# Turning q's features with VectorE's 32x32 transpose instead of TensorE, for seven of nine token blocks

## The chip, the cores and the metric

The kernel runs on one core of a Trainium2 chip. The metric is the device time of one execution in microseconds (us); less is better. A core has five engines that each run their own program in order and wait for one another through semaphores: TensorE (PE, matmuls; the profile lists its weight loads as PEld), VectorE (DVE), ScalarE (ACT), GpSimd (POOL) and SyncE (SP, which here only starts transfers).

## The reference

Three layers in float32, on inputs of batch 8, 8 heads, 576 positions, 64 features:

```python
q_s = exp(q - max(q, axis=-1)); q_s = q_s / (sum(q_s, axis=-1) + 1e-9)
k_s = exp(k - max(k, axis=2));  k_s = k_s / (sum(k_s, axis=2) + 1e-9)
kv = einsum('bhsd,bhse->bhde', k_s, v)
x = einsum('bhsd,bhde->bhse', q_s, kv)     # -> 4608 tokens x 512
h = x @ w_in;  g = where(h > 0, h, exp(min(h, 0)) - 1);  x = g @ w_out     # 512 -> 2048 -> 512
h = x @ w_in2; g = P(h) / (Q(h) + 1e-6);                 out = g @ w_out2  # P, Q: polynomials of h
```

The first line is the softmax of q over its 64 features, and it is the one that the change touches: for x, a token's 64 features have to lie on partitions (they are contracted with kv), while a maximum and a sum over features want them along the free axis.

## The kernel before

The 4608 tokens are nine blocks of 512 (index `j`, 0 to 8). Attention is done per pair of heads (`hp`, 0 to 3), so there are 36 units of q work, n = 4j + hp. Each matrix product of the two feed-forward layers is done as three matmuls on a high and a low part of each operand (L726 to L728 for `x @ w_in`, L768 for `g @ w_out`), each on tiles of 128x512. A step is one 128-wide slice of the hidden dimension: 12 matmuls into `h`, then on the first layer relu (ACT, L832), exp (ACT, L835), elu (DVE, L838), the high part (ACT, L269), the low part (POOL or DVE, L272), then 12 matmuls of L768. The tile `gs` of high and low part has two buffers; `h` takes one of four PSUM banks.

The q work of a pair (`pair_fns`, `plan_q`) in a 128x512 tile `qt`, with 128 tokens on the partitions and 4 tokens x 2 heads x 64 features along the free axis: `load_q` (SP), `q_max` (DVE, L480), `q_sub` (POOL, L483), `q_exp` (ACT, L487), `q_sum` (DVE, L491), `q_rec` (DVE, L494 and L495), `q_mul` (POOL, L498). Then `q_T`: four TensorE transposes of 128x128 into one PSUM bank (L504), and `q_copy` (ACT, L509), which brings that bank to the tile `qT`. For every second pair, `x_mm` (PE, L545) multiplies two `qT` tiles with their kv matrices, and `x_hi` and `x_lo` make the `xs` tiles that the first layer reads.

Blocks 0 and 1 are done ahead of and beside the first steps (`plan_pair`). For blocks 2 to 8, `plan_late` joins the TensorE part of three pairs in one operation, the `unit` (`plan_unit`): `q_T` of the present pair, the transposes of k's maxima for two later pairs (L442, L450), and the 10 small products that make kv (`kv_mm`, L464). For block 8, which has no k of its own, the unit holds `q_T` alone.

What stands where in each engine's program is set when the program is built, by a planner (class `Plan`). Each operation has an engine with an estimated cost, the operations that it follows, the buffers that it takes and frees, and a rank; the planner starts next what can start first by these costs, and the rank decides between equals. The ranks of the q work of pair n come from `at_step(n)`, counted in steps. The engines then run in that order, whatever the real durations are.

Of the kernel before, what the change touches and what calls it, by code (L numbers as in the profile page):

```python
# [161 lines left out]
def linear_attention_elu_rational(  # L162
# [239 lines left out]
    def pair_fns(n):  # L402
# [69 lines left out]
        def kv_div(e):  # L472
            if e == "ACT":
                nc.scalar.activation(out=kvd[n % 8], in_=b["pk"][:, 0:D], func=AF.Copy, scale=b["rs"])
            else:
                nc.vector.tensor_scalar(out=kvd[n % 8], in0=b["pk"][:, 0:D], scalar1=b["rs"], scalar2=None, op0=ALU.mult)

        def q_max(e):
            b["mx"] = at.tile([P, 8], F32, tag="mx", name="mx", bufs=4)
            nc.vector.tensor_reduce(out=b["mx"], in_=b["qt"], op=ALU.max, axis=AX.X)  # L480

        def q_sub(e):
            engine[e].tensor_tensor(out=b["qt"], in0=b["qt"], in1=b["mx"][:, :, None].to_broadcast([P, 8, D]),  # L483
                                    op=ALU.subtract)
# [140 lines left out]

    def plan_unit(n, q_ready=None):

# [19 lines left out]
        need, free, take = [in_ops[tiles[int(r)]]], [], ["bank"] if any(has) else []  # L647
        if has[0]:
# [9 lines left out]
        if q_ready:  # L658
            need.append(q_ready)
            free.append(("qt", mine["q_op"]))  # L660
            take += ["bank", "qT"]
        u = chain("unit", (PE(0.15 + 0.1 * has[0] + 0.1 * has[1] + 0.65 * has[2] + 0.4 * bool(q_ready)), unit, need, r + 1),
                  take=take, free=free, extra=0.2)
# [11 lines left out]
        if has[2]:  # L675
# [3 lines left out]
            done.append(o)  # L679
        if done:  # L680
            at_ops.append(op((("", 0.0),), lambda e: None, done, r, free=[("bank", u)]))
        if q_ready:
            at_ops.append(op((("", 0.0),), lambda e: None, [mine["qc"]], r, free=[("bank", u)]))

    def plan_late(j, hp):
        n = j * NP + hp
        if n == 2 * NP:
            for m in (n, n + 1):
                plan_k(m)
                plan_unit(m - 2)  # L690
        if n + 2 < B * NP:
            plan_k(n + 2)
        r = at_step(n)
        plan_unit(n, plan_q(n, r - 1, in_ops[tiles[int(r) - 1]], AHEAD))
        if hp % 2:
            plan_x(n, r, [state[n - 1]["qc"], state[n]["qc"]])
# [355 lines left out]
def _laid_out(name, a, np):  # L1052
# [49 lines left out]
```

## Time and profile before

| what | value |
|---|---|
| time, median of 3 runs (lowest to highest) | 1616.13 us (1616.03 to 1617.8) |
| time of the profiled execution | 1616.44 us |
| its span, first to last instruction | 1614.7 us |
| TensorE busy, share of the span | 1584.6 us, 98% |
| VectorE, ScalarE, GpSimd busy | 979.9, 1018.6, 772.0 us (61%, 63%, 48%) |
| mean granted TensorE clock | 0.995 of full speed |

The profiled execution takes 1.74 us more than its span, and lies 0.3 us above the median. The matmuls overlap one another, so the duration of one (mean 379 to 383 ns for 128x512) is longer than the distance from its start to the start of the next; what one costs TensorE is that distance.

### The profile page before, as it was taken

How to read it: one execution, taken by the hardware profiler on the slowest of the kernel's cores; microseconds unless marked ns; L12 is line 12 of the kernel's file. 1: busy time of each engine (PE TensorE's matmuls, PEld its weight loads, DVE VectorE, ACT ScalarE, POOL GpSimd, SP SyncE). 2: the span in 40 equal slices, each digit the busy share in tenths (PEclk: the TensorE clock that was granted, in tenths of full speed). 3: DMA queues.
4: the chain of work that ended last, by engine and by line, in shares of the span. 5: the costliest groups of instructions: out<-in, count | busy, mean ns of one | idle time of the engine just before them, and what ended most of it. 6: DMA issues, size and time to landing. Idle time of an engine off the chain costs nothing.

```text
span 1614.7 us, 21797 instructions
## 1 busy us (share of the span) xinstructions
PE 1584.6 (98%) x8040; PEld 1364.2 (84%) x8040; DVE 979.9 (61%) x1390; ACT 1018.6 (63%) x1688; POOL 772.0 (48%) x562
## 2 busy tenths in 40 slices
PE   6999999999999999999999999999999999999998
PEld 4788888888888888888888888888888888888886
DVE  7897655445344444321125777776868677777676
ACT  6766544454454544443557777777777777777675
POOL 3334333333233322333566666666566666666554
PEclk9999999999999999999999999999999999999999
DMA  8522533232233222110433010101000010100000
GB/s 322 203 118 89 166 120 103 100 114 86 102 102 115 85 92 81 61 40 14 124 93 103 8 53 1 52 1 39 15 26 28 20 34 10 43 8 21 1 27 26
DMA packets 48778, 114.82 MB, mean 71 GB/s; under 512 B 5664, under 2 KB 5664, under 8 KB 46624
## 3 DMA queue, kind: packets, MB, share of 16 engines
q1 hardware_dynamic: 48096, 112.10, 20.1%
q8 instruction: 63, 1.03, 0.3%
q10 hardware_dynamic: 576, 1.33, 0.2%
q14 instruction: 43, 0.35, 0.1%
HBM read 84.05 MB, written 29.36 MB: 70 GB/s over the span
## 4 chain that ended last, share of the span: by engine, by line
PE 87%; issue 4%; ACT 4%; DVE 2%; POOL 2%; DMA 1%; POOLq 0%; SPq 0%; DVEq 0%; ACTq 0%
PE acc L768 42%; PE ps L726 14%; PE ps L728 14%; PE ps L727 14%; POOL gs L272 2%; PE ps L464 1%; PE ps L545 1%; PE ps L504 1%; ACT p L871 1%; ACT s L867 1%; ACT m L877 0%; DMA hc<-w 0%; DMA kt<-in_k_dram 0%; ACT m L880 0%; PE acc L464 0%
## 5 line engine op out<-in xcount | busy, mean ns | idle before, releaser
L726 PE MATMUL ps<-xs,w_in 128*128 128x512 f32 x1152 | 438.8, 381 | 1.8 <-DVE p L892 1.7
L727 PE MATMUL ps<-xs,w_in 128*128 128x512 f32 x1152 | 436.6, 379 | 0.0
L728 PE MATMUL ps<-xs,w_in 128*128 128x512 f32 x1152 | 436.6, 379 | 0.0
L768 PE MATMUL acc<-gs,w_out 128*128 128x512 f32 x1728 | 407.1, 383 | 5.9 <-POOL gs L272 3.2
L272 POOL TENSOR_TENSOR gs<-m,gs 128x512 fp32r<-128x512 f32 x130 | 177.9, 1369 | 413.4 <-ACT gs L269 413.4
L768 PEld LDWEIGHTS acc<-gs,w_out 128*128 128x128 f32 x1728 | 324.9, 190 | 58.3 <-POOL gs L272 4.7
L838 DVE SCALAR_TENSOR_TENSOR m<-m,ps 128x512 f32<-128x512 f32 x144 | 98.9, 687 | 291.8 <-ACT m L835 278.9
L726 PEld LDWEIGHTS ps<-xs,w_in 128*128 128x128 f32 x1152 | 217.7, 189 | 37.2 <-issue 5.3
L728 PEld LDWEIGHTS ps<-xs,w_in 128*128 128x128 f32 x1152 | 217.7, 189 | 30.8
L727 PEld LDWEIGHTS ps<-xs,w_in 128*128 128x128 f32 x1152 | 217.7, 189 | 30.5
L874 POOL TENSOR_TENSOR s<-s,m 128x512 f32<-128x512 f32 x144 | 219.4, 1524 | 12.6 <-ACT m L863 12.6
L272 POOL TENSOR_TENSOR gs<-p,gs 128x512 fp32r<-128x512 f32 x72 | 116.1, 1613 | 211.7 <-issue 172.8
L768 PE MATMUL acc<-w_out,gs 128*128 128x512 f32 x864 | 200.9, 382 | 2.8 <-ACT gs L269 1.6
L768 PE MATMUL acc<-w_out,g 128*128 128x512 f32 x864 | 199.8, 379 | 0.5 <-POOL g L272 0.5
L832 ACT ACTIVATE m<-ps 128x512 f32<-128x512 f32 x144 | 85.8, 596 | 178.3 <-PE ps L728 122.5
L768 PEld LDWEIGHTS acc<-w_out,gs 128*128 128x128 f32 x864 | 164.3, 190 | 27.5 <-ACT gs L269 2.0
L768 PEld LDWEIGHTS acc<-w_out,g 128*128 128x128 f32 x864 | 163.2, 189 | 24.0 <-POOL g L272 0.9
L892 DVE SCALAR_TENSOR_TENSOR p<-p,a_sb,ps 128x512 f32<-128x512 f32 x144 | 107.5, 747 | 91.2 <-ACT m L863 91.1
L871 ACT ACTIVATE p<-ps,a_sb 128x512 f32<-128x512 f32 x144 | 112.2, 779 | 79.1 <-POOL gs L272 73.4
L269 ACT ACTIVATE gs<-m 128x512 fp32r<-128x512 f32 x144 | 90.4, 628 | 112.5 <-PE acc L768 97.7
L883 DVE SCALAR_TENSOR_TENSOR s<-s,m 128x512 f32<-128x512 f32 x144 | 135.4, 940 | 24.1 <-ACT m L880 23.9
L896 DVE SCALAR_TENSOR_TENSOR p<-p,a_sb,m 128x512 f32<-128x512 f32 x144 | 142.0, 986 | 2.3
(102 smaller groups left out, 1817.5 us busy)
## 6 DMA issues: line engine op xcount, KB each, us to landing
kt<-in_k_dram SPq DMA_DIRECT2D x32, 320.0 KB, 3.1
x<-e SPq DMA_DIRECT2D x36, 256.0 KB, 2.0
e<-x SPq DMA_DIRECT2D x36, 256.0 KB, 3.1
out_dram<-e SPq DMA_DIRECT2D x36, 256.0 KB, 2.0
vb<-in_v_dram SPq DMA_DIRECT2D x28, 325.0 KB, 3.4
bits<-in_moe_w_in_dram SPq DMA_DIRECT2D x8, 1024.0 KB, 10.3
qt<-in_q_dram SPq DMA_DIRECT2D x32, 256.0 KB, 3.2
bits<-in_moe_w_out_dram SPq DMA_DIRECT2D x8, 1024.0 KB, 11.9
```

The lines of the kernel that those rows point to most:

```text
L269: nc.scalar.activation(out=hi, in_=src, func=AF.Copy)
L272: engine[e].tensor_tensor(out=lo, in0=src, in1=hi.bitcast(F32), op=ALU.subtract)
L726: nc.tensor.matmul(o, w[:, 0, kk, :], two(x[:, 0]), start=(kk == 0), stop=False)
L727: nc.tensor.matmul(o, w[:, 0, kk, :], two(x[:, 1]), start=False, stop=False)
L728: nc.tensor.matmul(o, w[:, 1, kk, :], two(x[:, 0]), start=False, stop=(kk == KD - 1))
L768: nc.tensor.matmul(turned(o), lhsT, two(rhs), start=(f == f0 and n == 0), stop=(f == f1 and n == 2))
L838: nc.vector.scalar_tensor_tensor(out=b["m"], in0=b["m"], scalar=-1.0, in1=b["h"], op0=ALU.add, op1=ALU.max)
L871: nc.scalar.activation(out=b["p"], in_=b["h"], func=AF.Identity, scale=a_sb[:, 3:4], bias=a_sb[:, 2:3])
L874: engine[e].tensor_tensor(out=b["s"], in0=b["s"], in1=b["a"], op=ALU.add)
L883: nc.vector.scalar_tensor_tensor(out=b["s"], in0=b["s"], scalar=1.0 + 1e-6, in1=b["a"], op0=ALU.add, op1=ALU.mult)
L892: nc.vector.scalar_tensor_tensor(out=b["p"], in0=b["p"], scalar=a_sb[:, 1:2], in1=b["h"], op0=ALU.add, op1=ALU.mult)
L896: nc.vector.scalar_tensor_tensor(out=b["p"], in0=b["p"], scalar=a_sb[:, 0:1], in1=b["a"], op0=ALU.add, op1=ALU.mult)
```

## The change

For blocks 2 to 8 (28 of the 36 pairs) the host lays q out otherwise. A pair has 2 heads x 64 features, and each group of 32 partitions now holds a quarter of them: partitions 0 to 31 the first half of the first head's features, 32 to 63 its second half, and 64 to 127 the same of the second head. Along the free axis lie 16 groups of 32 features, one for each 32 of the block's 512 tokens. A row's maximum then is that of two halves which lie 32 partitions apart: `q_max` gives 128x16 halves, `swap` brings each group's halves beside those of its neighbour by four copies of 32x16 (on ACT or DVE, as the planner chooses), and `q_top` takes the larger. The sums are met in the same way (`q_swap2`, `q_rec2`). With this layout VectorE's transpose, which turns blocks of 32x32, gives the wanted `qT` in one instruction (`q_turn`); `q_T` and `q_copy` are gone for these pairs, and so is the PSUM bank that they took. The q work of a pair is also ranked two steps ahead of its unit instead of one (`EARLY`). `MOVE` holds the planner's costs for the four copies.

```diff
-            b["qt"] = qt.rearrange("p (n d) -> p n d", d=D)
+            b["qt"] = qt.rearrange("p (n d) -> p n d", d=D if j < 2 else D // 2)
...
+        nq = 8 if j < 2 else 16
+        dq = 8 * D // nq
+
         def q_max(e):
-            b["mx"] = at.tile([P, 8], F32, tag="mx", name="mx", bufs=4)
-            nc.vector.tensor_reduce(out=b["mx"], in_=b["qt"], op=ALU.max, axis=AX.X)
+            b["mx"] = b["sm"] = at.tile([P, 32], F32, tag="mx", name="mx", bufs=4)
+            nc.vector.tensor_reduce(out=b["mx"][:, 0:nq], in_=b["qt"], op=ALU.max, axis=AX.X)
+
+        def swap(e, t):
+            for i in range(4):
+                dst, src = t[i * 32:(i + 1) * 32, nq:2 * nq], t[(i ^ 1) * 32:(i ^ 1) * 32 + 32, 0:nq]
+                if e == "ACT":
+                    nc.scalar.activation(out=dst, in_=src, func=AF.Copy)
+                else:
+                    nc.vector.tensor_copy(out=dst, in_=src)
...
+        def q_top(e):
+            mx = b["mx"]
+            nc.vector.tensor_tensor(out=mx[:, 0:nq], in0=mx[:, 0:nq], in1=mx[:, nq:2 * nq], op=ALU.max)
...
+        def q_rec2(e):
+            sm = b["sm"]
+            nc.vector.scalar_tensor_tensor(out=sm[:, 0:nq], in0=sm[:, 0:nq], scalar=1e-9, in1=sm[:, nq:2 * nq], op0=ALU.add,
+                                           op1=ALU.add)
+            nc.vector.reciprocal(out=sm[:, 0:nq], in_=sm[:, 0:nq])
+
+        def q_turn(e):
+            b["qT"] = f32_tile("qT", 2, at)
+            nc.vector.transpose(out=b["qT"], in_=b["qt"].rearrange("p n d -> p (n d)"))
...
+    EARLY = 2
+    MOVE = (("ACT", 0.85), ("DVE", 0.65))
...
         o = chain("q_max", (DVE(0.67), b["q_max"], [lq, gate], r))
+        if n >= 2 * NP:
+            o = chain("q_swap", (MOVE, b["q_swap"], [o], r))
+            o = chain("q_top", (DVE(0.2), b["q_top"], [o], r))
         o = chain("q_sub", (either, b["q_sub"], [o], r))
         o = chain("q_exp", (ACT(0.65), b["q_exp"], [o], r + 0.1))
         o = chain("q_sum", (DVE(0.67), b["q_sum"], [o], r + 0.5))
+        if n >= 2 * NP:
+            o = chain("q_swap", (MOVE, b["q_swap2"], [o], r + 0.8))
+            o = chain("q_rec", (DVE(0.42), b["q_rec2"], [o], r + 1))
+            o = chain("q_mul", (either, b["q_mul"], [o], r + 1.2))
+            b["t_op"] = b["qc"] = o = chain("q_turn", (DVE(0.7), b["q_turn"], [o], r + 1.5), take=["qT"], free=[("qt", lq)],
+                                            extra=ahead)
+            return o
...
         def unit(e):
-            if q_ready:
-                mine["q_T"](e)
-            ps = bank() if any(has) else None
+            ps = bank()
...
         r = at_step(n)
-        plan_unit(n, plan_q(n, r - 1, in_ops[tiles[int(r) - 1]], AHEAD))
+        if n < B * NP:
+            plan_unit(n)
+        plan_q(n, r - EARLY, in_ops[tiles[int(r - EARLY)]], AHEAD)
...
+        early = a[:2].reshape(2, P, 4, h // 2, 2 * d).transpose(0, 3, 1, 2, 4).reshape(2, h // 2, P, 4 * 2 * d)
+        a = a[2:].reshape(-1, 4, 32, 4, h // 2, 2, 2, 32).transpose(0, 4, 5, 6, 2, 3, 1, 7).reshape(-1, h // 2, P, 4 * 2 * d)
+        a = np.concatenate([early, a])
```

Over the whole program this takes 112 transposes of L504 from PE and 28 copies of L509 from ACT. It adds 128 copies of 32x16 to ACT and 96 to DVE (32 and 24 swaps), and to DVE 28 each of `q_top`, the joining add and the transpose; 8 of the low parts of `gs` go from POOL to DVE. The number of transfers stays. The order on all engines is as before up to the first pair of block 2 (some 145 us into the span), and again through the second layer. In the pieces of order below, the changed kernel's line numbers are its own: L761 to L763 are L726 to L728 of before, L803 is L768, L867 and L870 are L832 and L835, L873 is L838, L483 is `q_max` (L480 before), L518 is `q_exp`, L521 is `q_sum` (L491 before).

On PE, the unit of block 2's first pair (between two runs of the first layer's matmuls); before:

```order
L768 MATMUL acc<-gs,w_out 128x512 x12
L504 MATMUL ps<-ident,qt 128x128 x4
L442 MATMUL ps<-ident,km 128x128
L450 MATMUL ps<-ident,top 128x128
L464 MATMUL ps<-vb,kt 64x65 x10
```

The same place with the change:

```order
L761 MATMUL ps<-xs,w_in 128x512
L762 MATMUL ps<-xs,w_in 128x512
L763 MATMUL ps<-xs,w_in 128x512
L442 MATMUL ps<-ident,km 128x128
L450 MATMUL ps<-ident,top 128x128
L464 MATMUL ps<-vb,kt 64x65 x10
```

The four transposes in front of L442 are gone, and the unit stands one run of L768 earlier; nothing takes the transposes' place.

On DVE, where block 2's first pair begins; before (`mx` and `sm` are the maxima and sums, `m` the first layer's hidden tile, `x` and `st` weights that are being converted):

```order
L438 TENSOR_REDUCE km<-kt 128x128
L480 TENSOR_REDUCE mx<-qt 128x8
L838 SCALAR_TENSOR_TENSOR m<-m,ps 128x512
L491 TENSOR_REDUCE sm<-qt 128x8
L494 TENSOR_SCALAR sm<-sm 128x8
L495 RECIPROCAL sm<-sm 128x8
L293 TENSOR_SCALAR st<-st 128x512
```

With the change:

```order
L483 TENSOR_REDUCE mx<-qt 128x16
L498 TENSOR_TENSOR mx<-mx 128x16
L873 SCALAR_TENSOR_TENSOR m<-m,ps 128x512
L272 TENSOR_TENSOR gs<-m,gs 128x512
L446 TENSOR_REDUCE top<-ps 128x1
L521 TENSOR_REDUCE mx<-qt 128x16
L453 TENSOR_TENSOR kt<-kt,ps 128x640
L505 SCALAR_TENSOR_TENSOR mx<-mx 128x16
L507 RECIPROCAL mx<-mx 128x16
L293 TENSOR_SCALAR st<-st 128x512
L297 TENSOR_SCALAR st<-st 128x512
L438 TENSOR_REDUCE km<-kt 128x128
L511 STREAM_TRANSPOSE qT<-qt 128x512
```

`q_top` (L498) stands in front of the elu of a step, and has to wait there for the copies on ACT; the transpose (L511) closes the pair's work.

On ACT at the same time, before:

```order
L269 ACTIVATE gs<-m 128x512
L832 ACTIVATE m<-ps 128x512
L835 ACTIVATE m<-m 128x512
L301 ACTIVATE x<-bits 128x1024
L269 ACTIVATE gs<-m 128x512
```

With the change:

```order
L269 ACTIVATE gs<-m 128x512
L867 ACTIVATE m<-ps 128x512
L489 ACTIVATE mx<-mx 32x16 x4
L870 ACTIVATE m<-m 128x512
L269 ACTIVATE gs<-m 128x512
L518 ACTIVATE qt<-qt 128x512
L489 ACTIVATE mx<-mx 32x16 x4
```

The four copies of a swap stand between a step's relu and its exp, with the elu and the high part behind them.

## Rows read from the trace of the kernel before

**Rows 1.** The page: span, and the engines' busy times.
```profile
span 1614.7 us, 21797 instructions
PE 1584.6 (98%) x8040; PEld 1364.2 (84%) x8040; DVE 979.9 (61%) x1390; ACT 1018.6 (63%) x1688; POOL 772.0 (48%) x562
```

**Rows 2.** Busy time by stretch: us, PE, PEld, DVE, ACT, POOL, clock, DMA.
```profile
0.00:115.00 115.00, 96.08 (x579) 76.13 (x580) 96.97 (x130) 79.61 (x118) 38.90 (x32) 0.94 0.58 226
115.00:140.00 25.00, 22.55 (x105) 19.12 (x104) 22.16 (x21) 17.05 (x25) 11.18 (x5) 1.00 0.15 53
140.00:760.00 620.00, 620.00 (x3458) 530.95 (x3457) 282.36 (x494) 303.30 (x516) 198.01 (x160) 1.00 0.28 94
```

**Rows 3.** PE's waits from 115 to 760 us: us in total, times, longest.
```profile
PE acc L768 <- POOL gs L272: 1.4, 1, 1.4
PE ps L442 <- DVE m L838: 1.0, 1, 1.0
```

**Rows 4.** Timeline of PE, a unit of block 4: start, us, instruction, count.
```profile
317.91 0.38 PE L728 MATMUL ps<-xs,w_in 128*128 128x512 f32 x1
318.13 0.60 PE L504 MATMUL ps<-ident,qt 128*128 128x128 f32 x4
318.57 0.27 PE L442 MATMUL ps<-ident,km 128*128 128x128 f32 x1
```

**Rows 5.** Timeline of PE, the last pair's transposes and the runs around.
```profile
743.33 2.75 PE L768 MATMUL acc<-gs,w_out 128*128 128x512 f32 x12
745.92 0.38 PE L726 MATMUL ps<-xs,w_in 128*128 128x512 f32 x1
...
748.51 0.60 PE L504 MATMUL ps<-ident,qt 128*128 128x128 f32 x4
748.86 2.84 PE L768 MATMUL acc<-gs,w_out 128*128 128x512 f32 x12
751.54 0.38 PE L726 MATMUL ps<-xs,w_in 128*128 128x512 f32 x1
```

**Rows 6.** Groups by line and shape, PE, 115 to 760 us: busy, mean ns.
```profile
L504 PE MATMUL ps<-ident,qt 128*128 128x128 f32 x112 | 16.8, 273 | 0.0
```

**Rows 7.** The same for DVE, 140 to 760 us.
```profile
L838 DVE SCALAR_TENSOR_TENSOR m<-m,ps 128x512 f32<-128x512 f32 x109 | 74.9, 687 | 234.8 <-ACT m L835 222.5 <-PE ps L464 8.2 <-issue 3.7
L480 DVE TENSOR_REDUCE mx<-qt 128x8 f32<-128x512 f32 x28 | 18.9, 675 | 0.0
L446 DVE TENSOR_REDUCE top<-ps 128x1 f32<-128x128 f32 x23 | 6.7, 290 | 22.6 <-PE ps L464 22.5
L469 DVE TENSOR_SCALAR rs<-ps 128x1 f32<-128x1 f32 x24 | 3.6, 148 | 6.3 <-PE ps L464 6.3
```

**Rows 8.** The same for ACT, 140 to 760 us.
```profile
L832 ACT ACTIVATE m<-ps 128x512 f32<-128x512 f32 x108 | 64.4, 597 | 148.5 <-PE ps L728 111.5 <-POOL gs L272 31.8 <-DVE gs L272 4.6
L509 ACT ACTIVATE qT<-ps 128x512 f32<-128x512 f32 x28 | 16.2, 580 | 0.0
L474 ACT ACTIVATE kvd<-ps,rs 128x64 f32<-128x64 f32 x24 | 7.5, 314 | 19.1 <-DVE kt L453 16.5 <-DVE sm L494 1.9 <-DVE rs L470 0.6
L1026 ACT ACTIVATE b_sb<-b_sb 128x1 f32<-128x1 f32 x1 | 0.2, 191 | 0.0
```

**Rows 9.** Timeline, all engines, one step's `gs` and its run of L768.
```profile
158.44 0.63 ACT L269 ACTIVATE gs<-m 128x512 fp32r<-128x512 f32 x1 [2.04 <-DVE m L838]
159.15 1.28 POOL L272 TENSOR_TENSOR gs<-m,gs 128x512 fp32r<-128x512 f32 x1 [0.27 <-ACT gs L269]
...
165.24 1.46 PE L768 MATMUL acc<-gs,w_out 128*128 128x512 f32 x6
```

**Rows 10.** Timeline, all engines, three runs of L768 back to back.
```profile
540.13 8.04 PE L768 MATMUL acc<-gs,w_out 128*128 128x512 f32 x36
...
543.03 0.63 ACT L269 ACTIVATE gs<-m 128x512 fp32r<-128x512 f32 x1
...
543.74 1.28 POOL L272 TENSOR_TENSOR gs<-m,gs 128x512 fp32r<-128x512 f32 x1 [2.89 <-ACT gs L269]
```

More of the change, by code (lines that the diff above doesn't have):

```diff
@@ L489, in q_sum @@
         def q_sum(e):
-            b["sm"] = at.tile([P, 8], F32, tag="sm", name="sm", bufs=4)
-            nc.vector.tensor_reduce(out=b["sm"], in_=b["qt"], op=ALU.add, axis=AX.X)
+            nc.vector.tensor_reduce(out=b["sm"][:, 0:nq], in_=b["qt"], op=ALU.add, axis=AX.X)
         def q_rec(e):
-            nc.vector.tensor_scalar(out=b["sm"], in0=b["sm"], scalar1=1e-9, scalar2=None, op0=ALU.add)
-            nc.vector.reciprocal(out=b["sm"], in_=b["sm"])
+            sm = b["sm"][:, 0:nq]
+            nc.vector.tensor_scalar(out=sm, in0=sm, scalar1=1e-9, scalar2=None, op0=ALU.add)
+            nc.vector.reciprocal(out=sm, in_=sm)
         def q_mul(e):
-            engine[e].tensor_tensor(out=b["qt"], in0=b["qt"], in1=b["sm"][:, :, None].to_broadcast([P, 8, D]),
+            engine[e].tensor_tensor(out=b["qt"], in0=b["qt"], in1=b["sm"][:, 0:nq, None].to_broadcast([P, nq, dq]),
                                     op=ALU.mult)
@@ L511, in pair_fns @@
         b.update({f.__name__: f for f in (load_k, load_v, load_q, k_max, k_maxT, k_top, k_row, k_sub, k_exp, kv_mm, kv_norm,
-                                          kv_div, q_max, q_sub, q_exp, q_sum, q_rec, q_mul, q_T, q_copy)})
-        return b
+                                          kv_div, q_max, q_sub, q_exp, q_sum, q_rec, q_mul, q_T, q_copy, q_swap, q_top, q_swap2,
+                                          q_rec2, q_turn)})
+        return b
+    EARLY = 2
+    MOVE = (("ACT", 0.85), ("DVE", 0.65))
     def plan_q(n, r, gate, ahead):
@@ L624, in plan_k, with plan_unit @@
         b["km_op"] = chain("k_max", (DVE(1.3), b["k_max"], [l, in_ops[tiles[int(r) - 1]]], r - 1), take=["km"], extra=AHEAD)
-    def plan_unit(n, q_ready=None):
+    def plan_unit(n):
         r = at_step(n)
@@ L645, in unit @@
                 b[2]["kv_mm"](e, ps)
-        need, free, take = [in_ops[tiles[int(r)]]], [], ["bank"] if any(has) else []
+        need, free, take = [in_ops[tiles[int(r)]]], [], ["bank"]
         if has[0]:
@@ L657, in plan_unit @@
             take.append("kvd")
[L658 to L662, printed above, removed]
+        u = chain("unit", (PE(0.15 + 0.1 * has[0] + 0.1 * has[1] + 0.65 * has[2]), unit, need, r + 1),
                   take=take, free=free, extra=0.2)
@@ L667, in plan_unit @@
             done.append(o)
-        if q_ready:
-            mine["t_op"] = u
-            mine["qc"] = chain("q_copy", (ACT(), mine["q_copy"], [u], r + 1.1), extra=AHEAD)
         if has[1]:
@@ L679, in plan_unit @@
             done.append(o)
[L680 to L683, printed above, removed]
+        at_ops.append(op((("", 0.0),), lambda e: None, done, r, free=[("bank", u)]))
     def plan_late(j, hp):
@@ L1057, in _laid_out @@
         b, h, s, d = a.shape
-        a = a.transpose(0, 2, 1, 3).reshape(b * s // TB, P, 4, h // 2, 2 * d).transpose(0, 3, 1, 2, 4)
-        a = a.reshape(b * s // TB, h // 2, P, 4 * 2 * d)
+        a = a.transpose(0, 2, 1, 3).reshape(b * s // TB, TB, h, d)
+        early = a[:2].reshape(2, P, 4, h // 2, 2 * d).transpose(0, 3, 1, 2, 4).reshape(2, h // 2, P, 4 * 2 * d)
+        a = a[2:].reshape(-1, 4, 32, 4, h // 2, 2, 2, 32).transpose(0, 4, 5, 6, 2, 3, 1, 7).reshape(-1, h // 2, P, 4 * 2 * d)
+        a = np.concatenate([early, a])
     elif name in ("k", "v"):
```

6 lines of the change are left out of this document (5 added, 1 removed).

## The prediction

> **What bounds the kernel now.** I read the page's head first: PE is busy for 1584.6 of 1614.7 us, and no other engine for more than 63% [rows 1]. Such a share is an average, so the second view is the busy time by stretch. There the reader is to see three regimes in the part that matters: up to 115 us PE is idle for 19 us in all, from 115 to 140 us for 2.4 us, and from 140 to 760 us it is busy for 620.00 of 620.00 us at full clock, while DVE works for 282 us of these, ACT for 303 and POOL for 198 [rows 2]. The third view, PE's waits, has only two short ones from 115 us on, 1.4 and 1.0 us [rows 3], which are the 2.4 us ahead of 140 us. The other way round, ACT's relu waited 111.5 us for PE's matmuls in this stretch, and DVE's elu 222.5 us for ACT [rows 8, 7]. So from 140 to 760 us the end is set by how many matmuls PE has to issue, and what is taken from PE there comes off the time whole, as long as nothing new makes PE wait. The transposes that the change removes all lie in that stretch: 112 of L504 between 115 and 760 us [rows 6], four for each of the 28 pairs.
>
> **What the removed transposes are worth.** The duration of one (273 ns on average, rows 6) is no price, since matmuls overlap. I take the distance between starts. In a unit of block 4 the matmul ahead starts at 317.91, the four transposes at 318.13, L442 behind them at 318.57 [rows 4]: 0.44 us for four, 0.11 each, with the usual 0.22 ahead of them. In block 8 the transposes stand alone between runs: they start at 748.51, the run of 12 behind them at 748.86, which is 0.35 us; but that run takes 2.68 us to the next matmul (751.54), where an undisturbed run takes 2.59 (743.33 to 745.92) [rows 5], so these cost 0.44 us too. 28 x 0.44 = **12.3 us**. Two other readings bound it from above: the busy time of the group, 16.8 us [rows 6], which counts the tail that overlaps the next matmul; and 112 durations end to end, 112 x 0.273 = 30.6 us, which the starts in rows 4 rule out as it stands. From below: nothing, if something else has to end last.
>
> The Trainium skill, "TensorE: Matmul & The Clock Gate", Part 4 (PE-mode transpose), tells of about 275 ns for a 128x128 transpose within a kernel, most of it access latency. This trace's 273 ns agrees as a duration; as a price it would make the sum 30.8 us.
>
> **What is added, and what hides it.** In 140 to 760 us:
> DVE gets 28 transposes of 128x512. The trace has none. The nearest row is a pass over the same 128x512 tile that reads once, `q_max` with 675 ns [rows 7]; I take that, with 19 us for 28, and as the other end four times that, 2.7 us each and 76 us in all. It gets 96 copies of 32x16, between 148 ns (128x1) and 290 ns (128x128 to 128x1) [rows 7]; I take 160, since 16 elements are nearest the small end: 15 us (14 to 28). `q_top` is as small, 28 x 0.17 = 5 us, the joining add takes the place of the add that was there, and 8 low parts moved from POOL are taken as an elu each, 8 x 0.69 = 5.5 us. Sum 45 us: DVE goes from 282 to 327 us of about 608, 54% (with the high ends 64%).
> ACT loses 28 copies of 580 ns, 16.2 us, and gets 128 of 32x16, between 191 ns (128x1) and 314 ns (128x64) [rows 8]; I take 200: 25.6 us (24 to 40). ACT goes from 303 to 313 us, 51%.
> POOL loses eight low parts, SP has the same transfers, only earlier.
> None of that is on PE, and with half of each engine's time free the work fits. A sum of busy time hides the order, though, so I look at two places where an insertion could reach PE.
>
> The first is `x_mm`, which now waits for `q_turn`. Counted in the changed order, the first such transpose pair of block 2 is closed behind the elu of step 22, and its `x_mm` stands behind the matmuls of step 26; in later blocks the distance is four to five steps as well. With 24 matmuls of 0.216 us a step is 5.2 us and four are 21; the elu and the transpose themselves end some 3 us behind the step's matmuls, so the chain could be over 15 us late before PE noticed.
>
> The second is each step's own chain, relu, exp, elu, high and low part, into whose queues the copies and the transpose are put: the fragment of ACT's order shows a swap between relu and exp, and that of DVE `q_top` ahead of the elu. Behind them wait the elu, then the high part, then L768 on PE. In an ordinary step the slack is large: the low part that starts at 159.15 ends at 160.43, and PE reads it at 165.24 [rows 9] (the run at 160.06 still reads the other buffer), 4.8 us. A swap of 0.8 us, a wait for it and a transpose of 0.7 us disappear in it. Where runs of L768 stand back to back it is small: of 36 matmuls from 540.13 us the third dozen starts at 540.13 + 24 x 0.216 = 545.31, and its low part ends at 543.74 + 1.28 = 545.02 [rows 10], 0.29 us before. A swap ahead of such a high part would cost PE 0.8 - 0.29 = 0.5 us. The changed order has 15 runs of two dozen or more between blocks 2 and 7, before there were 18. If each met one swap, that were 15 x 0.5 = 7.5 us; the planner places an operation where its costs say that nothing waits, and its costs are near the rows (0.85 us for a swap on ACT against 4 x 0.20, 0.7 for the transpose against 0.68), so I expect few of these, and put 0.2 us into the sum.
>
> The sum: 1616.44 (the profiled execution) - 12.3 + 0.2 = 1604.3. The median of the runs lies 0.3 us below that execution, so the forecast for the median is **1604.0 us**, 0.75% less. Up to 145 us the order is unchanged on all engines, so are PE's idle 21 us there, and the second layer's order is as before: I cost both at nothing.
>
> The page "VectorE: DVE Perf Modes" of the Trainium skill (The three transpose paths, and Rules for kernel authors) speaks against the move: a whole 128x128 transpose is to go to TensorE where PSUM will do as its place, and VectorE's 32x32 blocks are given with 311 ns for 128x128 in bf16. An estimate from that page is 4 x 0.311 = 1.24 us for a `q_turn`, or 35 us for 28; no run here shows it yet.
>
> **The rivals.**
> *Back-to-back runs give part of it back.* Mechanism and price as above: up to 7.5 us, so 1604 to 1611.5. For it: 0.29 us of slack [rows 10]. Against it: PE had no wait of this kind between 140 and 760 us, though 18 such runs stood there [rows 2, 3].
> *The transposes were worth more than their spacing:* 16.8 us by their busy time gives 1616.1 - 16.8 = 1599.3, and 30.6 us by their durations 1585.5. Against it: the starts [rows 4, 5].
> *Hidden anyway, no change:* if DVE or ACT really paced the steps, PE would only wait instead, at 1616. Against it: ACT and DVE wait for PE, and not PE for them [rows 3, 7, 8].
> *Slower: VectorE's transpose is many times slower than a pass.* DVE works in order, so the elu behind each of the 28 transposes is late by what a transpose takes beyond 0.68 us, and so are the high part, the low part and L768. The ordinary slack of 4.8 us swallows the first part. With a transpose of T us PE loses T - 5.5 on each; to lose the 12.3 us again takes 0.44 more, T = 5.9 us, and over 0.2% slower begins at T = 6.0 (28 x 0.55 = 15.5 us); at T = 7 it is 1604 + 42 = 1646. For it: the trace holds no transpose on DVE. Against it: it would have to be nine times the 675 ns of the nearest pass [rows 7].
>
> **Chances and range.** A time differs measurably from 1616.1 when it differs by over 0.2%, 3.2 us; the runs of before spread by 1.8. Forecast, with up to 2 us of new waits: 82%, 1602.5 to 1606. Back-to-back waits of 2 to 7.5 us: 8%. Worth more: 4%. No change: 3%. Slower: 3%. Faster is 82 + 8 + 4 less a little of the second case, 93%; same 4%, slower 3%. The range takes the forecast and half of the second case, 1601.8 to 1607.5.
>
> **What would show it.** L504 only 32 times (four e and four qt pairs); PE still 100% busy from 140 us to about 748; the first matmul of layer two some 12 us earlier. `q_turn` between 0.6 and 1.3 us, a copy of a swap about 0.16 us on DVE and 0.2 on ACT; DVE at about 54% and ACT at 51% there. Wrong would show as waits of L768 for `gs` in runs of two dozen, as waits of L545 for DVE, or as PE's spacing around the unit changing otherwise than by 0.44 us.

## The result and the profile after

The changed kernel takes 1602.22 us (median of 4 runs, 1601.73 to 1605.11) against 1616.27 us of the kernel before beside it: ratio 0.9915, 95% interval 0.9898 to 0.9932. Run once more (experiment e12 below, 5 runs), it takes 1605.98 us against 1616.84, ratio 0.9930 (0.9918 to 0.9943). The forecast was 1604.0, faster, 1601.8 to 1607.5. So the sign, the size and both medians lie where the prediction put them; what makes the two measurements differ by 4 us was not in it, and is half of what follows.

The head of the changed kernel's page, to be held against [rows 1]: TensorE has 112 instructions less, VectorE has 50 us more work.

```profile
span 1600.4 us, 21856 instructions
PE 1570.7 (98%) x7928; PEld 1350.9 (84%) x7928; DVE 1030.3 (64%) x1550; ACT 1030.3 (64%) x1788; POOL 760.0 (47%) x554
```

The busy time by stretch of the changed kernel (columns as in [rows 2]). PE is still busy from 140 us to the end of the first layer's q work, 607.96 of 608.00 us at full clock, though DVE now works 331 us of these:

```profile
140.00:748.00 608.00, 607.96 (x3346) 518.74 (x3345) 331.15 (x654) 314.72 (x615) 185.50 (x152) 1.00 0.28 95
```

PE's waits of the changed kernel from 115 us to the end of the program, for [rows 3]. There is none for the transposed tile (a wait of L590, `x_mm`), and those of L803 for `gs` lie ahead of 140 us and in the last 15 us of the program:

```profile
PE acc L803 <- POOL gs L272: 2.4, 2, 1.4
PE ps L761 <- DVE p L927: 1.6, 1, 1.6
PE acc L803 <- ACT gs L269: 1.6, 1, 1.6
PE ps L442 <- DVE m L873: 0.9, 1, 0.9
PE acc L803 <- POOL g L272: 0.5, 1, 0.5
```

The timeline of PE in a unit of the changed kernel, for [rows 4]: L442 starts 0.22 us behind the matmul ahead of it, with nothing between them.

```profile
314.30 0.38 PE L763 MATMUL ps<-xs,w_in 128*128 128x512 f32 x1
314.52 0.27 PE L442 MATMUL ps<-ident,km 128*128 128x128 f32 x1
```

The new work on DVE from 130 to 760 us, in groups by line and shape (L511 is the transpose, L491 a copy of a swap, L483 `q_max`, L498 `q_top`), and on ACT (L489, a copy of a swap). The transpose costs about what a pass over the tile costs, 707 ns beside the 680 of `q_max`:

```profile
L511 DVE STREAM_TRANSPOSE qT<-qt 128x512 f32<-128x512 f32 x28 | 19.8, 707 | 13.5 <-POOL qt L529 8.5 <-PE ps L590 4.9
L491 DVE COPY mx<-mx 32x16 f32<-32x16 f32 x96 | 20.2, 211 | 1.8
L483 DVE TENSOR_REDUCE mx<-qt 128x16 f32<-128x512 f32 x28 | 19.0, 680 | 0.0
L498 DVE TENSOR_TENSOR mx<-mx 128x16 f32<-128x16 f32 x28 | 5.3, 190 | 6.2 <-ACT mx L489 6.0
...
L489 ACT ACTIVATE mx<-mx 32x16 f32<-32x16 f32 x128 | 27.3, 213 | 10.2 <-DVE mx L521 4.7 <-DVE mx L483 3.6
```

The 211 ns of L491 are a mean of two kinds. Of the 96 copies on DVE 90 take 161 to 171 ns, and four stand in 0.70 us. The other six take 0.51 to 1.29 us; each of these runs beside a low part on POOL (L272) and ends 0.03 us behind it. The timeline has first an ordinary swap, then one that meets POOL:

```profile
361.89 0.70 DVE L491 COPY mx<-mx 32x16 f32<-32x16 f32 x4
...
295.26 1.83 DVE L491 COPY mx<-mx 32x16 f32<-32x16 f32 x4
295.43 1.28 POOL L272 TENSOR_TENSOR gs<-m,gs 128x512 fp32r<-128x512 f32 x1 [5.06 <-ACT gs L269]
```

**Where the time came from.** I cut every trace at the same three instructions of PE: the first `x @ w_in` matmul of step 18 (shortly ahead of the first change of order), the first of step 144 (layer two), and the last one of the program. The first two in the trace of before:

```profile
139.12 0.38 PE L726 MATMUL ps<-xs,w_in 128*128 128x512 f32 x1
...
853.76 0.38 PE L726 MATMUL ps<-xs,w_in 128*128 128x512 f32 x1
```

and in that of the changed kernel:

```profile
138.69 0.38 PE L761 MATMUL ps<-xs,w_in 128*128 128x512 f32 x1
...
841.41 0.38 PE L761 MATMUL ps<-xs,w_in 128*128 128x512 f32 x1
```

853.76 - 139.12 = 714.64 us became 841.41 - 138.69 = 702.72: the stretch that the change touches gave **11.92 us**. The whole span fell by 14.3. The same cut for every kernel of this study (us, from each profiled execution; "behind it" is the span, rounded to 0.1 us, less the start of the last `x @ w_in` matmul):

| kernel | to step 18 | step 18 to 144 | 144 to the last x@w_in | behind it | span |
|---|---|---|---|---|---|
| before | 139.12 | 714.64 | 735.31 | 25.63 | 1614.7 |
| changed | 138.69 | 702.72 | 735.23 | 23.76 | 1600.4 |
| changed, again (e12) | 139.78 | 702.72 | 735.43 | 26.67 | 1604.6 |
| e1 spare transposes | 139.14 | 713.19 | 737.69 | 25.28 | 1615.3 |
| e2 one transpose of four | 138.85 | 705.79 | 737.59 | 23.87 | 1606.1 |
| e3 turn x4 | 139.11 | 709.65 | 737.79 | 26.75 | 1613.3 |
| e4 turn x9 | 140.24 | 759.70 | 735.24 | 25.72 | 1660.9 |
| e5 one step ahead | 139.75 | 702.65 | 735.21 | 25.19 | 1602.8 |
| e6 before, tail filled | 139.25 | 714.65 | 735.46 | 23.84 | 1613.2 |
| e7 changed, tail filled | 140.19 | 702.72 | 735.21 | 23.78 | 1601.9 |
| e8 swaps on DVE | 140.38 | 703.10 | 735.21 | 27.61 | 1606.3 |
| e9 the same, tail filled | 140.24 | 702.92 | 737.78 | 24.76 | 1605.7 |
| e10 start filled | 137.71 | 702.71 | 737.69 | 25.49 | 1603.6 |
| e11 start and tail filled | 137.51 | 702.73 | 737.67 | 23.79 | 1601.7 |

The second column repeats to 0.1 us wherever the q work is the same, on three occasions and whatever the median. Of the other three, the start varies by up to 1.7 us between kernels without a fill there, layer two by 2.6 and the tail by 3.9. Two executions of one program (changed and e12) differ by 1.1, 0.2 and 2.9 us.

**What varies in the tail is TensorE's granted clock.** The last waits of PE in the trace of before, by the timeline:

```profile
1598.54 2.42 PE L768 MATMUL acc<-w_out,g 128*128 128x512 f32 x10 [0.46 <-POOL g L272]
1602.57 0.70 PE L768 MATMUL acc<-w_out,gs 128*128 128x512 f32 x2 [1.60 <-ACT gs L269]
1604.30 4.11 PE L768 MATMUL acc<-w_out,gs 128*128 128x512 f32 x10 [1.03 <-POOL gs L272]
```

in the changed kernel:

```profile
1585.98 2.43 PE L803 MATMUL acc<-w_out,g 128*128 128x512 f32 x10 [0.46 <-POOL g L272]
1590.00 0.70 PE L803 MATMUL acc<-w_out,gs 128*128 128x512 f32 x2 [1.59 <-ACT gs L269]
1591.72 2.43 PE L803 MATMUL acc<-w_out,gs 128*128 128x512 f32 x10 [1.02 <-POOL gs L272]
```

and in the changed kernel run again:

```profile
1587.28 2.43 PE L803 MATMUL acc<-w_out,g 128*128 128x512 f32 x10 [0.46 <-POOL g L272]
1591.30 0.70 PE L803 MATMUL acc<-w_out,gs 128*128 128x512 f32 x2 [1.59 <-ACT gs L269]
1593.03 4.63 PE L803 MATMUL acc<-w_out,gs 128*128 128x512 f32 x10 [1.03 <-POOL gs L272]
```

The waits are the same to 0.01 us, but the ten matmuls behind them take 4.11, 2.43 and 4.63 us. The busy time by stretch of the last of these traces shows the granted clock (behind the five engines) falling in the last wait and then standing at 0.50, that is 1.2 GHz, while PE is busy for 4.57 of 4.60 us:

```profile
1591.00:1593.00 2.00, 0.70 (x2) 0.30 (x2) 1.93 (x3) 0.25 (x1) 1.58 (x1) 0.80 0.00 0
1593.00:1597.60 4.60, 4.57 (x11) 3.67 (x12) 1.22 (x2) 0.63 (x1) 0.00 (x0) 0.50 0.00 0
```

In the first measurement's trace the clock stayed at 1.00 over that place. So 1.87 us of its 14.3 are a tail that happened to run at 2.4 GHz. Of the ten traces without a fill in the tail (e6, e7, e9 and e11 have one) two kept the clock there, the changed kernel's and e2's; in the other eight the ten matmuls take 3.82 to 4.63 us. In e8 and e9 there is something besides the clock: the program ends 4.6 and 4.7 us behind its last matmul, in all others 3.7.

### The profile page after: what moved, and what is told of

It is laid out like the page before. It is cut to its first block, busy times and chain, and to the rows that moved or that the text cites. A ratio compares the mean times of both kernels' runs of the same rounds, so it can differ in the third digit from the quotient of the medians.

```text
span 1600.4 us, 21856 instructions
## 1 busy us (share of the span) xinstructions
PE 1570.7 (98%) x7928; PEld 1350.9 (84%) x7928; DVE 1030.3 (64%) x1550; ACT 1030.3 (64%) x1788; POOL 760.0 (47%) x554
## 4 chain that ended last, share of the span: by engine, by line
PE 88%; ACT 4%; issue 4%; DVE 2%; POOL 2%; DMA 1%; POOLq 0%; SPq 0%; DVEq 0%; ACTq 0%
PE acc L803 43%; PE ps L761 14%; PE ps L763 14%; PE ps L762 14%; POOL gs L272 2%; PE ps L464 1%; PE ps L590 1%; ACT p L906 1%; ACT s L902 1%; ACT m L912 0%; ACT m L915 0%; PE acc L464 0%; DMA hc<-w 0%; PE ps L535 0%; DMA e<-in_q_dram 0%
## 5 line engine op out<-in xcount | busy, mean ns | idle before, releaser
L761 PE MATMUL ps<-xs,w_in 128*128 128x512 f32 x1152 | 438.1, 380 | 1.8 <-DVE p L927 1.6
L763 PE MATMUL ps<-xs,w_in 128*128 128x512 f32 x1152 | 436.6, 379 | 0.0
L803 PE MATMUL acc<-gs,w_out 128*128 128x512 f32 x1728 | 409.0, 383 | 5.6 <-POOL gs L272 3.1
L803 PEld LDWEIGHTS acc<-gs,w_out 128*128 128x128 f32 x1728 | 324.6, 190 | 58.7 <-POOL gs L272 4.9
L272 POOL TENSOR_TENSOR gs<-m,gs 128x512 fp32r<-128x512 f32 x122 | 167.9, 1376 | 356.3 <-ACT gs L269 354.0
L761 PEld LDWEIGHTS ps<-xs,w_in 128*128 128x128 f32 x1152 | 217.7, 189 | 36.8 <-issue 5.2
L763 PEld LDWEIGHTS ps<-xs,w_in 128*128 128x128 f32 x1152 | 217.7, 189 | 30.8
L873 DVE SCALAR_TENSOR_TENSOR m<-m,ps 128x512 f32<-128x512 f32 x144 | 98.6, 685 | 224.3 <-ACT m L870 219.9
L272 POOL TENSOR_TENSOR gs<-p,gs 128x512 fp32r<-128x512 f32 x72 | 116.4, 1616 | 211.2 <-issue 171.9
L803 PE MATMUL acc<-w_out,gs 128*128 128x512 f32 x864 | 199.2, 379 | 2.7 <-ACT gs L269 1.6
L803 PE MATMUL acc<-w_out,g 128*128 128x512 f32 x864 | 199.8, 379 | 0.5 <-POOL g L272 0.5
L867 ACT ACTIVATE m<-ps 128x512 f32<-128x512 f32 x144 | 85.8, 596 | 161.8 <-PE ps L763 122.9
L803 PEld LDWEIGHTS acc<-w_out,gs 128*128 128x128 f32 x864 | 163.1, 189 | 26.9 <-ACT gs L269 2.0
L803 PEld LDWEIGHTS acc<-w_out,g 128*128 128x128 f32 x864 | 163.2, 189 | 24.0 <-POOL g L272 0.9
L269 ACT ACTIVATE gs<-m 128x512 fp32r<-128x512 f32 x144 | 90.4, 628 | 102.0 <-PE acc L803 86.5
L924 DVE TENSOR_TENSOR p<-p,ps 128x512 f32<-128x512 f32 x144 | 98.2, 682 | 73.8 <-issue 57.0
```

What stands on the lines that cost most here:

```text
L269: nc.scalar.activation(out=hi, in_=src, func=AF.Copy)
L272: engine[e].tensor_tensor(out=lo, in0=src, in1=hi.bitcast(F32), op=ALU.subtract)
L761: nc.tensor.matmul(o, w[:, 0, kk, :], two(x[:, 0]), start=(kk == 0), stop=False)
L763: nc.tensor.matmul(o, w[:, 1, kk, :], two(x[:, 0]), start=False, stop=(kk == KD - 1))
L803: nc.tensor.matmul(turned(o), lhsT, two(rhs), start=(f == f0 and n == 0), stop=(f == f1 and n == 2))
L873: nc.vector.scalar_tensor_tensor(out=b["m"], in0=b["m"], scalar=-1.0, in1=b["h"], op0=ALU.add, op1=ALU.max)
```

## The experiments

**e1: the transposes back on TensorE, without use.** In the changed kernel:

```diff
             ps = bank()
+            if has[2]:
+                for _ in range(4):
+                    nc.tensor.transpose(ps[:, 3 * P:4 * P], ident, ident)
```

> The changed kernel with four idle TensorE transposes of the identity put back at the head of each of the 24 units that still exist (into a free corner of the unit's PSUM bank, read by nobody, the planner's costs and so every order otherwise as in the changed kernel). Theory, what a transpose costs is the distance between starts: 24 x 0.44 = 10.6 us more than the changed kernel, 1612.8, and the last matmul of x @ w_in later by just that. Rival, what counted was something else that went with them (the PSUM bank, the copy on ScalarE, the order): 0 to 3 us more. Rival, durations: 24 x 4 x 0.273 = 26 us more. The end after the last matmul of x @ w_in (25.6 us in the profile before, 23.8 after) may take either value, as TensorE's clock there stays up or falls.

Measured: 1617.24 us (10 runs, 1615.92 to 1618.37; before beside it 1616.77), ratio 1.0004 (0.9995 to 1.0013). The stretch of steps 18 to 144 goes from 702.72 to 713.19, +10.47 us for 24 times four: 0.436 us for four, 0.109 each. The timeline of PE shows one such group:

```profile
318.24 0.38 PE L766 MATMUL ps<-xs,w_in 128*128 128x512 f32 x1
318.46 0.60 PE L685 MATMUL ps<-ident 128*128 128x128 f32 x4
318.89 0.27 PE L442 MATMUL ps<-ident,km 128*128 128x128 f32 x1
```

Of the 14.9 us between the two spans the other 4.4 lie elsewhere, 2.46 in layer two, 1.5 in the tail and 0.45 at the start; the table has such values for kernels without the spare transposes too. In layer two PE waits longest at one place, for PSUM (for `p`, a step of the rational function), in the changed kernel

```profile
872.30 0.45 PE L761 MATMUL ps<-xs,w_in 128*128 128x512 f32 x1 [1.64 <-DVE p L927]
```

and in e1

```profile
883.99 0.45 PE L764 MATMUL ps<-xs,w_in 128*128 128x512 f32 x1 [2.85 <-DVE p L930]
```

with a granted clock of 0.69 behind it, by stretch:

```profile
885.00:890.00 5.00, 5.00 (x17) 4.04 (x17) 3.12 (x5) 4.82 (x9) 3.51 (x3) 0.69 0.14 52
```

In the table this place has two values. Where the longest of these waits is 1.64 us or less, layer two takes 735.2 to 735.5 us; in the six traces where it is 2.72 to 2.85 us (e1, e2, e3, e9, e10, e11), the clock falls and it takes 737.6 to 737.8.

The traces tell the two apart earlier. Some 17 us into layer two ACT converts a piece of `w_out` that a transfer brings (`w_out<-hc`, L269). SP issues that transfer 12.9 us after the first matmul of step 144 in all 14 traces. In the eight with the short wait ACT has to wait for its landing by 1.07 to 1.59 us, in the six with the long one by 0.86 us or not at all. From there on ACT, POOL and DVE meet in another order in time, and `s<-s,m` and `m<-s,m`, two operations of DVE ahead of the one that PE waits for, take 0.68 and 0.69 us in the eight and some 1.77 and 1.63 in the six. Timeline of ACT and of DVE in the changed kernel:

```profile
858.84 0.63 ACT L269 ACTIVATE w_out<-hc 128x512 fp32r<-128x512 f32 x1 [1.07 <-DMA hc<-w]
...
870.77 0.69 DVE L921 SCALAR_TENSOR_TENSOR m<-s,m 128x512 f32<-128x512 f32 x1
```

and in e1, where ACT does not wait:

```profile
868.59 0.61 ACT L269 ACTIVATE w_out<-hc 128x512 fp32r<-128x512 f32 x1
...
881.55 1.63 DVE L924 SCALAR_TENSOR_TENSOR m<-s,m 128x512 f32<-128x512 f32 x1
```

So weights that land later go with a layer two that is some 2.4 us shorter. That holds in all 14 traces, but no run moved the transfer: it is an association, and not shown as a cause.

**e2: three of four transposes left out of the kernel before.** ACT's copy reads the one four times, so three quarters of q are missing from the output for blocks 2 to 8.

```diff
-            for i in range(4):
+            for i in range(4 if j < 2 else 1):
...
```

> The kernel before with one of the four transposes per pair of blocks 2 to 8 (the copy to qT reads that one four times, so three quarters of q are left out; every engine's order, bank use and ScalarE's work as before). Theory, TensorE alone: 28 x 3 x 0.11 = 9.2 us less than before, 1607.0. Rival, part of the gain came from the freed bank, the missing copies or the new order: clearly less than 9.2 us. The end after the last matmul of x @ w_in takes 25.6 or some 23.9 us, and moves the time by up to 1.7 us.

Measured: 1608.50 us (4 runs, 1606.89 to 1610.3), ratio 0.9950 (0.9936 to 0.9965). The stretch falls from 714.64 to 705.79, 8.85 us for 84 transposes, 0.105 each, without any of VectorE's new work. Layer two has the long wait and gives 2.3 back.

**e3 and e4: VectorE's transpose done four and nine times.**

```diff
-            nc.vector.transpose(out=b["qT"], in_=b["qt"].rearrange("p n d -> p (n d)"))
+            for _ in range(4):       # e4: range(9)
+                nc.vector.transpose(out=b["qT"], in_=b["qt"].rearrange("p n d -> p (n d)"))
```

> The changed kernel with every transpose on VectorE done four times (28 x 3 x 0.71 = 60 us more work on VectorE, the planner knows nothing of it). Theory, VectorE has slack in each step (4.8 us in an ordinary one, 0.3 before runs back to back): 0 to 3 us more, 1602 to 1605. Rival, VectorE is close to pacing the steps: over 10 us more.

> The changed kernel with every transpose on VectorE done nine times, 6.4 us in place of 0.71. By the working of the prediction a transpose of T us costs TensorE T - 5.5 on each of the 28: 28 x 0.9 = 25 us more, 1627. If the steps' slack is larger than the 4.8 us read in one of them, less; if a transpose mostly stands ahead of runs back to back, up to 28 x 5.4 = 150 us more.

Measured: e3 1613.49 us (10 runs, 1608.66 to 1615.12), ratio 0.9974 (0.9964 to 0.9983); e4 1662.32 us (4 runs), ratio 1.0280 (1.0264 to 1.0295). Both are slower than expected: the stretch lost 6.93 us at 2.8 us a turn, and 56.98 us at 9 x 0.711 = 6.4 us. The profiled execution of e3 is the slowest of its ten, which spread over 6.5 us; what the stretch lost in the others is not known. In e3 5.2 us of the loss fall between steps 30 and 32, at one place. The timeline there, of DVE, ACT and PE in turn:

```profile
202.38 2.95 DVE L512 STREAM_TRANSPOSE qT<-qt 128x512 f32<-128x512 f32 x4
...
205.98 0.67 DVE L483 TENSOR_REDUCE mx<-qt 128x16 f32<-128x512 f32 x1
...
206.69 0.91 ACT L489 ACTIVATE mx<-mx 32x16 f32<-32x16 f32 x4 [5.01 <-DVE mx L483]
209.02 0.63 ACT L519 ACTIVATE qt<-qt 128x512 f32<-128x512 f32 x1 [1.42 <-POOL qt L515]
209.55 0.61 ACT L269 ACTIVATE gs<-m 128x512 fp32r<-128x512 f32 x1
...
210.22 0.48 PE L804 MATMUL acc<-gs,w_out 128*128 128x512 f32 x1 [2.23 <-ACT gs L269]
211.63 6.92 PE L804 MATMUL acc<-gs,w_out 128*128 128x512 f32 x23 [0.93 <-POOL gs L272]
```

A swap on ACT waits 5.01 us for the next pair's `q_max`, which is queued behind the four transposes; the exp of q stands behind the swap and waits for POOL's subtraction, and the step's high part stands behind both. PE waits 3.16 us for `gs`, and then its clock is at 0.67 for 5 us. At the same place in the changed kernel the swap waits for 2.80 us and the high part has slack to spare, since it waits 1.89 us for PE:

```profile
199.64 0.91 ACT L489 ACTIVATE mx<-mx 32x16 f32<-32x16 f32 x4 [2.80 <-DVE mx L483]
201.98 0.63 ACT L518 ACTIVATE qt<-qt 128x512 f32<-128x512 f32 x1 [1.42 <-POOL qt L514]
204.50 0.63 ACT L269 ACTIVATE gs<-m 128x512 fp32r<-128x512 f32 x1 [1.89 <-PE acc L803]
```

In e4 the waits spread over many lines; the two longest rows of PE's waits from 140 to 815 us are

```profile
PE ps L762 <- DVE xs L272: 10.7, 5, 3.5
PE ps L591 <- DVE m L874: 5.8, 3, 3.8
```

**e5: the q work ranked one step ahead** (`EARLY = 1`), as before the change.

> The changed kernel with EARLY = 1, q's work ranked one step ahead of the unit, as before, instead of two. Theory: x_mm has four steps (over 15 us) of slack behind the transpose, so one step less changes nothing: 1602 to 1603. Rival, the earlier rank is what keeps the longer chain from being late: several us more, as waits of L590 for VectorE.

Measured: 1604.02 us (4 runs, 1602.84 to 1604.57), ratio 0.9920 (0.9906 to 0.9933). The stretch takes 702.65 us: the earlier rank earns nothing, as expected. The median is 1 us past the expected 1602 to 1603. Against the first trace of the changed kernel the start is 1.06 us longer, and the tail 1.4 us, which are the clock's again (the ten matmuls take 3.82 us).

**e6 and e7: TensorE's last two waits filled,** in the kernel before and in the changed one:

```diff
+            def spare(n):
+                t = bank()
+                w = slot[f, 0].rearrange("p s (k c) -> p s k c", c=P)
+                for _ in range(n):
+                    nc.tensor.matmul(turned(t), w[:, 0, 0, :], two(x_tile[L, j, 0][:, 0]), start=True, stop=True)
...
+                late_one = L == 1 and j == NB - 1 and f == KF - 2
+                if late_one:
+                    spare(6)
...
+                        if late_one and i == 0 and n == 2:
+                            spare(4)
```

> The kernel before with ten idle matmuls put into TensorE's last two waits: six ahead of the second last slice's run of L768 (a wait of 1.6 us), four behind its first two matmuls (a wait of 1.0 us), into a free PSUM bank, read by nobody. Theory, the profiled execution of before lost 1.7 us at the end because the granted clock fell to half after those waits, and the waits are why: the clock stays at 1.00 to the end and the time is 1.7 us less, 1614.5. Rival, the fall has another cause (or the idle matmuls delay the end): 1616, or some tenths more.

> The changed kernel with the same ten idle matmuls. Theory: its clock stayed up at the end anyway in the profiled execution, so 0 to 0.3 us of difference there, 1602.2; but executions in which it falls (as the one of 1605.1 may have been) should be gone. Rival: they delay the end, up to 1 us more.

Measured: e6 1615.36 us (11 runs, 1614.85 to 1618.52) against 1616.84 without the fill, ratio 0.9995 (0.9986 to 1.0004): as a time no proof. The tail shows it: 23.84 us in e6, 23.78 in e7, as in the two unfilled traces that kept their clock (23.76 and 23.87), against 25.63 in before. e7 takes 1602.49 us (4 runs, 1602.04 to 1603.7), ratio 0.9912 (0.9899 to 0.9926). With both tails at 2.4 GHz the two kernels are 12.87 us apart by their medians, and 11.3 by the two profiled executions, of which e7's has a start longer by 0.94.

**e8 and e9: all swaps on VectorE,** first alone, then with the tail filled:

```diff
-    MOVE = (("ACT", 0.85), ("DVE", 0.65))
+    MOVE = (("DVE", 0.65),)
```

> The changed kernel with all 56 swaps on VectorE (224 copies there, none on ScalarE). Theory: neither engine paces the stretch, so no change, 1602 to 1603; a copy takes some 0.17 us there and starts only as the one ahead of it ends (four in 0.70 us). Rival, ScalarE's or VectorE's queue ahead of the elu matters: over 2 us either way.

> The changed kernel with all its small copies on VectorE, and ten idle matmuls (into a PSUM bank that nobody reads) in TensorE's last two waits of 1.6 and 1.0 us. Theory (the copies cost nothing; the 5.7 us that all copies on VectorE seemed to cost were the granted clock after the last waits, 3.85 us, and at the start, 1.3 us): all matmuls of the last group at 2.4 GHz, some 24 us from the last x@w_in matmul to the end, median 1602.5 to 1604.5. Rival (the copies on VectorE do hold up TensorE by some us): it stays at 1607 to 1608.

Measured: e8 1607.92 us (4 runs, 1604.37 to 1608.32), ratio 0.9938 (0.9923 to 0.9953), by its median a clear miss of the expected 1602 to 1603. But its stretch takes 703.10 us, 0.38 more than with the mixed swaps; the rest of the 5.9 us of span is 1.69 at the start and 3.85 in the tail. Of these 2.9 are the clock's (ten matmuls in 4.63 us, and the twelve behind them in 3.54 instead of 2.75), and 0.9 lie behind the last matmul. e9's median is 1605.11 us (5 runs, 1603.15 to 1607.58), ratio 0.9926 (0.9913 to 0.9940), just past its range. Its timeline shows the last waits shortened by the fill and the ten matmuls at full speed,

```profile
1594.30 0.70 PE L814 MATMUL acc<-w_out,gs 128*128 128x512 f32 x2 [0.30 <-ACT gs L269]
...
1596.03 2.43 PE L814 MATMUL acc<-w_out,gs 128*128 128x512 f32 x10 [0.17 <-POOL gs L272]
```

but this execution met the long wait of layer two (737.78), and its tail is 1.0 us longer than e7's behind the last matmul, as e8's is; what that time is stays open. To have the 32 swaps of ACT on VectorE as well costs the stretch 0.2 to 0.4 us.

**e10, e11 and e12: the start filled, start and tail filled, and the changed kernel again.** In e10 and e11 TensorE gets idle work in its waits of the first 43 us (`spare` as above):

```diff
+            if n == 3:
+                for _ in range(20):
+                    nc.tensor.transpose(b["tp"][0][:, 0:P], ident, ident)
...
+                        if (L, j, f, i) == (0, 0, 0, 0):
+                            spare((3, 5, 8)[n])
```

> The changed kernel with TensorE kept busy in five of its waits of the first 43 us: 20 idle transposes before the fourth k_turn (a wait of 2.4 us) and 3, 5 and 8 idle matmuls before the first three matmuls of the first g@w_out group (waits of 0.7, 1.1 and 1.8 us). Theory (the half-speed stretches at 25 to 31 us and 40 to 48 us follow from these waits): the clock stays at 2.4 GHz there, the twelve g@w_out matmuls stand 0.22 us apart and not 0.43, step 1 begins 2.0 to 2.6 us earlier, and the median is 1599.5 to 1600.5; what the first stretch gains (2.4 us) is swallowed by the waits for gs and w_out behind it. Rival (the start waits for loads and for the other engines): step 18 begins as before, and the median stays at 1602.

> The changed kernel with idle matmuls in the waits of the start and in the last two. Theory (both losses are of the clock alone): as with the start filled, with no run more than 1.5 us above the fastest, median 1599.5 to 1600.5. Rival (a fill only moves the fall of the clock to another wait): no gain over the changed kernel, 1602 to 1604.

> The changed kernel once more, unaltered, on the same chip as the three others, to see how often its last matmuls run at the lower clock. Theory (a chance of the moment): most runs 1601.7 to 1602.5 and some 1604 to 1606, the latter with a mean clock of 0.994; median 1602.2. Rival (the changed kernel keeps its clock at the end for a reason of its own): all runs 1601.7 to 1602.5.

Measured: e10 1604.67 us (5 runs, 1603.31 to 1605.38), ratio 0.9923 (0.9911 to 0.9935); e11 1603.40 us (4 runs, 1603.0 to 1605.3), ratio 0.9918 (0.9905 to 0.9932); e12 1605.98 us (5 runs, 1604.81 to 1606.42). The fill does what it should to the clock. Busy time from 20 to 50 us in the changed kernel and then in e11:

```profile
20.00:50.00 30.00, 22.69 (x139) 15.87 (x138) 27.55 (x44) 20.26 (x33) 11.97 (x9) 0.77 0.71 275
```

```profile
20.00:50.00 30.00, 26.83 (x202) 20.15 (x203) 28.33 (x44) 21.03 (x34) 11.81 (x9) 1.00 0.76 294
```

Step 18 begins at 137.71 and 137.51 us against 139.78 in e12, 2.1 to 2.3 us earlier, as expected of the theory; against the first trace of the changed kernel (138.69) it is 1.0 to 1.2. But both profiled executions then meet the long wait in layer two, and lose 2.3 us there. The expected 1599.5 to 1600.5 was missed by 3 to 4 us, and the intervals of e10 to e12 overlap: that the fills make a better kernel is not shown.

e12 was to tell how often the tail falls. Its median is neither the expected 1602.2 nor within the rival's 1601.7 to 1602.5. Its profiled execution reaches step 18 1.09 us later than the first trace of the changed kernel and takes 2.9 us longer in the tail. The tails of its other runs are not known, and the mean clock does not tell them: e12's runs have 0.994 and 0.995, but so has e7's profiled execution (0.994), whose tail ran at full speed. So the changed kernel does not keep its clock for a reason of its own; how often it keeps it is not shown.

## Why the prediction held, step by step

- **Price of the transposes, 28 x 0.44 = 12.3 us: right.** e1 gives 0.436 for four (28 x 0.436 = 12.2), e2 0.42 (11.8). The distance between starts was the price. Busy time (16.8 us) and durations end to end (30.6 us) were not: putting 96 of 112 back cost 10.5 us. The Trainium skill, "TensorE: Matmul & The Clock Gate", Part 4, has about 275 ns for a 128x128 transpose within a kernel; the trace agrees with that as a duration (273 ns, [rows 6]), and e1's 109 ns decides against it as a price.
- **New waits, 0.2 us: right in that there are hardly any.** 12.2 less the measured 11.92 leaves 0.3, and 11.8 leaves nothing, so 0.2 and zero can't be told apart. No wait of PE stands in the 608 us from 140 us on, although the 15 back-to-back runs do that were counted; the rival that priced these at up to 7.5 us did not come about.
- **Cost of the added work.** The transpose was taken as 675 ns and took 707. The Trainium skill, "VectorE: DVE Perf Modes", The three transpose paths, gave an estimate of 1.24 us for it, from its bf16 figure; the measured 707 ns decides. That page's advice (Rules for kernel authors) to send a 128x128 transpose to TensorE is about whole transposes. With the new layout only blocks of 32x32 have to be turned, and here, where TensorE is the bound, taking the whole ones from it gave 11.92 us. The copies took 213 ns on ACT where 200 were taken, and 211 on DVE where 160 were; 160 fits the 90 that do not meet POOL. DVE's share of 331 of 608 us is the forecast 54%, ACT's is 52%. None of it reached PE in the changed kernel and in e5; in e8, with all swaps on VectorE, 0.4 us did. The high end of DVE's share is misadded: 282 + 76 + 28 + 5 + 5.5 = 396 us are 65% of 608 and not 64%.
- **The slow-transpose rival had the right form but the wrong price.** It let PE lose T - 5.5 us on each of 28 and broke even at T = 5.9. e3 lost 6.9 us of the gain at T = 2.8, and e4 lost 57 at T = 6.4, where the formula gives nothing and 28 x 0.9 = 25. The step that failed was to follow only the elu behind the transpose. The next pair's `q_max` is queued there as well, ACT's swap waits for that, and the step's high part is behind the swap. A straight line between the two runs puts the break-even near T = 3.2 us; that is an estimate, from one execution each. At 707 ns the place that cost e3 most still has 1.89 us to spare.
- **Start, layer two and tail, costed at nothing: not right.** Their order did not change, but their time did, by -2.4 us in the first measurement (14.3 - 11.92) and by +1.8 in e12 (start +0.66, layer two +0.12, tail +1.04). Around 1604 these make 1602 and 1606. The prediction had no term for the clock, though it stands at 0.94 up to 115 us [rows 2] and the trace of before has ten matmuls in 4.11 us in the tail. So part of the hit is luck: the first median, 1602.22, lies below the 1602.5 to 1606 that stood for the forecast itself, and within the range only by 0.7 us at its lower end for which the prediction gives no reason; the second, 1605.98, lies at the upper end of that band.

What stays open: what decides at the tail, with equal waits to 0.01 us, whether the clock falls; and in layer two, why the transfer lands earlier in some executions and what makes the two operations of DVE longer then. The wait of layer two was not filled: it is a wait for a PSUM bank, and I take it that none is free then for idle matmuls to write to, which was not tried.

## What to carry to other kernels

An operation on the bounding engine costs the distance between starts, not its duration; an engine with half of its time free could take it over here, because one instruction does the work there in about the time of one pass. Follow the queue behind an inserted instruction to its second and third link: the slack that counts is that of the last thing queued, here the high part on ACT three links from the transpose on DVE. And cut the traces at the same instructions on the bounding engine before a difference in medians is explained: here the stretch that the change touches repeated to 0.1 us while the medians of one unaltered program lay 4 us apart.

## What the hardware showed that I had not expected

After three waits of PE of 0.46, 1.59 and 1.03 us, with work between them, the clock was at 1.2 GHz (0.50) for the next 4.6 us in one execution (e12) and at 2.4 GHz in another of the same program, at a cost of up to 2.9 us in the tail. After the single waits of 2.72 to 2.85 us in layer two it fell each of six times; after those of up to 1.64 us there it did not. Idle matmuls in the waits kept it at 2.4 GHz in the tail (e6, e7, e9, e11) and at the start (e10, e11). A copy of 32x16 to the neighbouring 32 partitions takes ScalarE some 210 ns and VectorE 0.17 us, a quarter to a third of the 707 ns of the whole 128x512 transpose; six of VectorE's 96 copies ended only with the operation of POOL that they met, after up to 1.29 us.
